# Two units of 1024 tokens, behind four units of 512: an H3 convolution layer interleaved with a squared-ReLU MLP

## The chip, the cores and the metric

The kernel runs on one core of a Trainium2 chip. The metric is the device time of one execution, in microseconds (us), as the median of several runs. The engines are named as in the profile: PE is TensorE, DVE is VectorE, ACT is ScalarE, POOL is GpSimd, SP is SyncE, which issues nearly all DMAs. "PEld" is the weight load of TensorE.

## What is computed

The reference, cut to what matters (S = 2048 tokens, D = 1024, F = 3584, everything float32):

```python
def A(u, k, v, shift_k, ssm_k, ssm_D):        # u = layernorm(x)
    k_shift = sum(k_pad[:, t:t + S] * shift_k[:, 3 - t] for t in range(4))
    kv = k_shift * v
    y = causal_conv(kv, ssm_k)                # per channel, as long as the sequence (by FFT)
    return u * (y + kv * ssm_D)
def B(u, w1, b1, w2, b2):
    return relu(u @ w1 + b1) ** 2 @ w2 + b2

x = A_q
for _ in range(2):                            # the same weights, and the same y, in both layers
    x = x + A(layernorm(x), ...)
    x = x + B(layernorm(x), ...)
```

## The kernel before

**Units.** The tokens are cut into four blocks of 512. The MLP of one layer for one block is a *unit*, and ORDER (L36) lists the eight of them as (layer, block): (0,0), (1,0), (0,1), (0,2), (1,1), (0,3), (1,2), (1,3). A float32 product is made of two rounded halves of each operand with three matmuls (mm3, L343 to L346: high by high, high by low, low by high), each 128x128 by 128x512. A *step* is one weight tile of 128x512: four mm3, or 12 matmuls. All steps stand in one list, and the program walks it (from about L2150); what is to happen beside the matmuls is hung on it: `lag.at(k, fn)` calls a function k steps later, generators (`prep_a`, `prep_rows`, `make_t`, the convolution's streams) are advanced by so much per step.

**Three sorts of unit.** A plain unit takes 112 steps (1344 matmuls): first w1 by the normalised rows of x, then relu2 (L1584), which squares and splits into rh and rl, then w2. Units 0 to 4 are plain. Unit 5, named by JU, is *joint* (add_joint, L934): the blocks (0,3) and (1,2) share each weight, as the two rows of a 2x2 block product done with 7 products instead of 8. Its first half ("ja", 98 steps) is w1 in 14 pairs of F tiles: products 1 and 2 of two pairs at a time, then products 6, 5, 7, 4, 3 from pair to pair. Product 1's bank is copied away (j_p1, L1905, tile fx) before the same banks are used on for the next product. Its second half ("jb", 98 steps) is w2 in the order JORD, with the left operands read back from HBM (r_load, r_hi, r_lo, walked by r_advance) and each finished product added into accumulators (j_evict). The sums of w1 tiles are made on the way (part_sums, L1045); the sums of w2 tiles (T) are made ahead by the generator make_t (L1599) and kept in HBM (TD). A joint unit is 196 steps (2352 matmuls). The last unit, (1,3), has a form of its own (WINO, add_wino L918): w1 in full, and 7 of 8 products of w2 within its 512 tokens; 1260 matmuls. `j_next` prepares its rows while the joint unit ends (late stage: transposes on PE, hi and lo copies, L2046 to L2049, from tiles yh).

**The convolution.** y is the same in both layers, and so is computed once, block by block, on the side. Its forward transforms (fwd_x, fwd_g; fwd_stream) are matmuls and butterflies, its products a stream (prod_stream, L528): POOL multiplies two spectra over j+1 blocks of 128 (`mult`, L532 to L534, tile cp, 128x384 to 128x1024 while unit 0 and later ones run), DVE sums over the blocks (`red`, L538, tile sm), POOL folds (fold, L683) and turns (butterfly, L686 to L689), DVE splits (L570), PE transforms back, and the result goes to HBM (yd). The stream is paced: `pace` gives each unit so much of it per step, such that block sb is done when unit WIN[sb] prepares its rows; `close_conv` forces what is left. Block 3 is not needed before unit 5, and so the convolution runs until 1700 us, in unit 4. After it make_t begins (L2380 or so).

**Rows.** prep_a and prep_b load and normalise the next unit's rows; prep_rows (L879) does so for the second block of a joint unit (layer norm, gate, layer norm), the statistics being kept in tiles rn. The bias b2 is added by POOL to the four accumulators of a unit, each 128x1024, one after the other (add_b2, L1829 to L1831).

**Weights.** They come eight steps ahead from HBM, raw (wr<-w, then split by ACT at L1103 and DVE at L1111) or as pairs split earlier (whl<-wd_m).

Of the kernel before, what the change touches and what calls it, by code (L numbers as in the profile page):

```python
# [3 lines left out]

# [22 lines left out]
FC = 7  # L27
# [30 lines left out]
JOPEN = (0, 4, 1)  # L58
JSUM = {0: ((0, 0),), 4: ((1, 1),), 5: ((0, 1),), 2: ((0, 1),), 1: ((0, 0),), 6: ((1, 1),), 3: ((1, 0),)}
J_PREP, J_SUMS, J_RATE = 22, 3, 1.1  # L60
R_LOAD, R_HI, R_LO = 8, 4, 3
W_PREP, W_EARLY, W_LATE = 90, (87, 80, 45, 38), 30
T_KEPT, T_RATE, T_AT = 10, 0.6, (0, 3, 1, 2)
WCH = (3, 3, 4, 4)
WHALF = T // 2
WORD, WORD_END = (0, 1, 3, 4, 5, 6, 2), (0, 3, 5, 6, 4, 2, 1)
WEND = {0: (), 3: (), 5: ((1, 1, 5, 0),), 6: ((1, 1, 6, 5), (2, 1, 3, 6), (2, 0, 3), (3, 1, 6, "x"), (3, 1, 1, 0)),
        4: ((1, 1, 6, 4), (1, 0, 6), (2, 1, 5, 4), (2, 1, 2, 5)), 2: ((1, 0, 2),), 1: ((1, 0, 1),)}
# [8 lines left out]
FWD_RATE = {0: 1.4, 1: 1.4, 2: 1.4, 3: 1.1, 4: 1.1, 5: 1}  # L77
# [171 lines left out]
def tile_h3_mlp(ctx: ExitStack, tc: tile.TileContext, q, kT, vT, shk, ssmT, ssmD, w1, b1, w2, b2,  # L249
# [97 lines left out]

    def hold(n):
        got = take(n)
        while not got:  # L350
            yield
            got = take(n)
        return got
# [8 lines left out]
    def fwd_x(sb, c):  # L362
# [14 lines left out]
        for _ in range(4 if sb == 1 else 7):  # L377
            yield
# [12 lines left out]
        yield  # L391
        give(o)
        yield
# [19 lines left out]
        yield  # L413
# [24 lines left out]
    def fwd_g(sb, c):  # L438
# [9 lines left out]
        if sb > PLAIN:  # L448
            hi = mkfg([P, T], F32R)
            lo = mkfg([P, T], F32R)  # L450
            A.copy(hi, raw)
            yield
            V.tensor_sub(lo, raw, hi.bitcast(F32))
            yield
            yield
            yield
# [38 lines left out]
        if sb <= PLAIN:  # L495
            yield
            yield
# [30 lines left out]
    def prod_stream():  # L528
# [3 lines left out]
        def mult(st, xt, gt, j):  # L532
            pr = cv.tile([P, CU, j + 1], F32, name="cp", bufs=3)
            G.tensor_mul(pr.rearrange("p c i -> p i c"), xt[:, 0:j + 1], gt[:, j::-1])  # L534
            st["pr"] = pr
# [4 lines left out]
        def fin(st, sm, sb, g, k):  # L540
# [24 lines left out]
            elif k == 3:  # L565
# [6 lines left out]
                if g % 2:  # L572
                    lag.at(1, fin, st, sm, sb, g, 4)
# [109 lines left out]
    def fold(E, s):  # L683
        E.tensor_add(s[:, 1:3], s[:, 1:3], s[:, 0:1].to_broadcast([P, 2, s.shape[2]]))  # L684
# [137 lines left out]
    def prep_w(l, b, lag):  # L822
        mv, r = lnx.pop((l, b))
        xT = []
        sts = [{} for _ in range(NT)]

        def early(tt, k):
            st = sts[tt]
            if k == 0:
                st["x"] = load_x(l, b, tt)  # L830
                st["y"] = pre.tile([P, D], F32, name="px", bufs=2)
                SY.dma_start(st["y"], YD[b][:, tt])
            elif k == 1:
                combine(st["x"], st.pop("y"), mv[:, tt, 0:1], r[:, tt:tt + 1])
            elif k == 2:
                st["mv"] = pre.tile([P, 1, 2], F32, name="mv2", bufs=4)
                stats(st["x"], st["mv"][:, 0])
                st["ve"], st["sd"] = rstd_a(st["mv"])
            elif k == 3:
                SY.dma_start(X1[b][:, tt], st.pop("x"))  # L840
                st["r"] = rstd_b(st["ve"], st["sd"])
                st["nr"] = pre.tile([P, 1], F32, name="nr", bufs=4)
                V.scalar_tensor_tensor(st["nr"], st["mv"][:, 0, 0:1], -1.0, st["r"], op0=OP.mult, op1=OP.mult)

        def late(tt, k):
            st = sts[tt]
            if k == 0:
                st["x"] = pre.tile([P, D], F32, name="px", bufs=2)
                SY.dma_start(st["x"], X1[b][:, tt])
            elif k == 1:  # L850
                for h in range(2):
                    sl = slice(h * 512, (h + 1) * 512)
                    A.activation(st["x"][:, sl], st["x"][:, sl], AF.Identity, bias=st["nr"], scale=st["r"])
            elif k == 2:
                if not xT:
                    xT.extend(mw.tile([P, KT, T], F32R, name=nm, bufs=1) for nm in ("xh", "xl"))
                st["o"] = []
                for kh in range(2):
                    o = ps1()
                    for c in range(4):  # L860
                        n = 4 * kh + c
                        PE.transpose(o[:, c * P:(c + 1) * P], st["x"][:, n * P:(n + 1) * P], ident)
                    st["o"].append(o.rearrange("p (k t) -> p k t", k=4))
            else:
                for kh in range(2):
                    hi, lo = (x[:, 4 * kh:4 * kh + 4, tt * P:(tt + 1) * P] for x in xT)
                    if k == 3:
                        A.copy(hi, st["o"][kh])
                    else:
                        V.tensor_sub(lo, st["o"][kh], hi.bitcast(F32))  # L870

        for tt in range(NT):
# [1551 lines left out]
```

## Time and profile before

| | us |
|---|---|
| median of 3 runs | 2679.24 |
| lowest, highest | 2675.58, 2681.99 |
| the profiled execution, its time | 2678.93 |
| its span in the trace | 2677.1 |
| PE busy | 2621.7 |
| DVE busy | 1987.5 |
| ACT busy | 1116.0 |
| POOL busy | 851.7 |
| DMA | 759.28 MB on the main queue |

The units follow one another in the trace at these times: the first convolution block until 126 us, then unit 0 (126 to 503), unit 1 (to 845), unit 2 (to 1179), unit 3 (to 1511), unit 4 (to 1828), the joint unit 5 (to 2385) and the last unit (to 2677). A row of the view by windows has the stretch, its length, then for PE, PEld, DVE, ACT and POOL the busy time with the count of instructions that fall in it, then the granted clock, the busy share of the DMA engines and GB/s. A row of the view of waits names an engine and line, what it waited for, the total in us, how many times, and the longest. A row of the view of one line has the count and the shortest, median and longest duration in ns.

### The profile page before, as it was taken

What the parts mean: (1) busy time and instruction counts of PE and PEld (TensorE: products, weight loads), DVE (VectorE), ACT (ScalarE), POOL (GpSimd) and SP (SyncE); (2) the same over time, 40 slices, a digit from 0 to 9 for tenths busy, and PEclk for the clock granted to TensorE, in tenths of its full rate; (3) what the DMA queues carried; (4) which work ended last, traced back from release to release, by engine and by line L of the source; (5) the groups of instructions that cost most, each with busy time, mean ns of one, the idle gap of its engine ahead of it and who ended that gap; (6) DMA issues with size and microseconds to landing.
All of it is one profiled execution on the core that took longest, in us unless ns stands there. A gap on an engine that the chain in (4) does not pass through costs nothing.

```text
span 2677.1 us, 36183 instructions
## 1 busy us (share of the span) xinstructions
PE 2621.7 (98%) x12400; PEld 2195.7 (82%) x12400; DVE 1987.5 (74%) x2993; ACT 1116.0 (42%) x1947; POOL 851.7 (32%) x532
## 2 busy tenths in 40 slices
PE   7999999999999999999999999999999999999999
PEld 7888787888888888888888888887787888788887
DVE  7879888789887877779777777655788674745565
ACT  4454344434444333343333422345655443345443
POOL 2336665355642645427554275100000030001000
PEclk9999999999999999999999999999999999999999
DMA  8789898689989898888987888777899988746556
GB/s 259 260 301 313 294 307 282 240 294 374 339 296 317 315 337 299 267 306 307 337 298 257 308 301 315 266 243 285 304 308 303 367 296 310 265 164 197 174 171 206
DMA packets 390680, 761.59 MB, mean 284 GB/s; under 512 B 45392, under 2 KB 160736, under 8 KB 390496
## 3 DMA queue, kind: packets, MB, share of 16 engines
q1 hardware_dynamic: 390496, 759.28, 82.4%
q8 instruction: 98, 1.61, 0.2%
q14 instruction: 86, 0.70, 0.1%
HBM read 581.92 MB, written 177.21 MB: 284 GB/s over the span
## 4 chain that ended last, share of the span: by engine, by line
PE 76%; DVE 9%; DMA 8%; issue 2%; SPq 2%; ACT 2%; POOL 1%; DVEq 0%; ACTq 0%; POOLq 0%
PE p L344 22%; PE p L345 22%; PE p L346 22%; DMA wr<-w 3%; PE p L1189 2%; PE pt L345 2%; PE pt L344 2%; PE pt L346 2%; DVE whl L1111 1%; DMA whl<-wd_m 1%; DMA cx<-xd 1%; DMA cg<-gd 0%; DVE st L705 0%; SPq L1955 0%; PE pt L429 0%
## 5 line engine op out<-in xcount | busy, mean ns | idle before, releaser
L534 POOL TENSOR_TENSOR cp<-cx,cg 128x384 f32<-128x384 f32 (+5 forms) x288 | 546.1, 1909 | 572.0 <-DVE sm L538 367.0
L344 PE MATMUL p<-xh,whl 128*128 128x512 f32 (+1 forms) x1504 | 576.8, 384 | 4.8 <-ACT fx L1907 2.9
L346 PE MATMUL p<-xh,whl 128*128 128x512 f32 (+1 forms) x1504 | 572.4, 381 | 0.8 <-POOL whl L1111 0.8
L345 PE MATMUL p<-xl,whl 128*128 128x512 f32 (+1 forms) x1504 | 572.4, 381 | 0.1
L1111 DVE TENSOR_TENSOR whl<-wr,whl 128x512 fp32r<-128x512 f32 x535 | 452.2, 858 | 95.6 <-ACT whl L1103 82.6
L1103 ACT CAST whl<-wr 128x512 fp32r<-128x512 f32 x550 | 334.7, 618 | 383.0 <-PE p L346 243.8
L344 PE MATMUL p<-whl,rh 128*128 128x512 f32 x1204 | 475.5, 395 | 3.8 <-ACT whl L1103 2.8
L345 PE MATMUL p<-whl,rh 128*128 128x512 f32 x1204 | 470.7, 391 | 1.3 <-POOL whl L1111 0.8
L346 PE MATMUL p<-whl,rl 128*128 128x512 f32 x1204 | 470.4, 391 | 0.0
L344 PEld LDWEIGHTS p<-xh,whl 128*128 128x128 f32 x1504 | 283.5, 189 | 59.5 <-ACT fx L1907 4.6
L346 PEld LDWEIGHTS p<-xh,whl 128*128 128x128 f32 x1504 | 283.1, 188 | 55.3 <-POOL whl L1111 1.0
L345 PEld LDWEIGHTS p<-xl,whl 128*128 128x128 f32 x1504 | 283.3, 188 | 52.3 <-DVE xl L1502 0.3
L344 PEld LDWEIGHTS p<-whl,rh 128*128 128x128 f32 x1204 | 227.3, 189 | 50.8 <-ACT whl L1103 3.8
L345 PEld LDWEIGHTS p<-whl,rh 128*128 128x128 f32 x1204 | 227.3, 189 | 48.1 <-DVE whl L1111 1.6
L346 PEld LDWEIGHTS p<-whl,rl 128*128 128x128 f32 x1204 | 226.9, 188 | 47.7
L1596 DVE TENSOR_TENSOR rl<-wr,rh 128x512 fp32r<-128x512 f32 x140 | 140.2, 1002 | 165.5 <-ACT rh L1591 165.5
L538 DVE TENSOR_REDUCE sm<-cp 128x128 f32<-128x384 f32 (+5 forms) x288 | 249.8, 874 | 11.4 <-POOL cp L534 11.4
L1588 ACT ACTIVATE wr<-p,b1t 128x512 f32<-128x512 f32 x138 | 95.2, 690 | 356.5 <-PE p L346 355.5
L2036 POOL TENSOR_TENSOR acc<-acc,px 128x512 f32<-128x512 f32 x8 | 11.7, 1481 | 454.0 <-DMA wr<-td 451.0
L1711 DVE TENSOR_TENSOR acc<-p,acc 128x512 f32<-128x512 f32 x152 | 99.8, 686 | 74.5 <-PE p L346 74.5
L684 POOL TENSOR_TENSOR sm<-sm 128x512 f32<-128x512 f32 x48 | 69.1, 1440 | 130.6 <-DVE sm L538 117.8
L1688 POOL TENSOR_TENSOR acc<-acc,px 128x512 f32<-128x512 f32 x6 | 7.7, 1318 | 267.6 <-DMA px<-b 267.6
(431 smaller groups left out, 4233.8 us busy)
## 6 DMA issues: line engine op xcount, KB each, us to landing
whl<-wd_m SPq DMA_DIRECT2D x334, 512.0 KB, 5.5
wr<-w SPq DMA_DIRECT2D x440, 256.0 KB, 5.4
wd_m<-whl SPq DMA_DIRECT2D x70, 512.0 KB, 6.2
wr<-td SPq DMA_DIRECT2D x104, 256.0 KB, 4.5
cx<-xd SPq DMA_DIRECT2D x48, 512.0 KB, 6.2
cg<-gd SPq DMA_DIRECT2D x48, 512.0 KB, 7.1
rh<-rd SPq DMA_DIRECT2D x84, 256.0 KB, 5.8
gd<-fg SPq DMA_DIRECT2D x72, 256.0 KB, 6.2
```

What stands on the lines that cost most here:

```text
L344: PE.matmul(o, lh, rh, start=start, stop=False, skip_group_check=skip)
L345: PE.matmul(o, lh, rl, start=False, stop=False, skip_group_check=skip)
L346: PE.matmul(o, ll, rh, start=False, stop=stop, skip_group_check=skip)
L534: G.tensor_mul(pr.rearrange("p c i -> p i c"), xt[:, 0:j + 1], gt[:, j::-1])
L538: V.tensor_reduce(sm[:, ty, jj], st["pr"], axis=AX.X, op=OP.add)
L684: E.tensor_add(s[:, 1:3], s[:, 1:3], s[:, 0:1].to_broadcast([P, 2, s.shape[2]]))
L1103: A.copy(t[:, 0], raws[n]["t"])
L1111: ENG[e[n % len(e)]].tensor_sub(t[:, 1], raws[n]["t"], t[:, 0].bitcast(F32))
L1189: PE.matmul(o, lh, r, start=start, stop=stop)
L1588: A.activation(r, st["o"], AF.Relu, bias=b1t[:, st["f"]:st["f"] + 1])
L1596: V.tensor_sub(st["lo"], st["r"]["t"], st["hi"].bitcast(F32))
L1711: V.tensor_add(accs[tt][:, d], o, accs[tt][:, d])
```

## The change

ORDER becomes (0,0), (1,0), (0,1), (0,2), (0,3), (1,1), (1,3), (1,2). Units 0 to 3 are plain as before, and behind them stand two joint units: JS = (4, 6), the blocks (0,3) with (1,1), and (1,3) with (1,2). The form of the last unit and all its functions (add_wino, prep_w, relu_w, evict_w, merge_w, store_w) are gone. In matmuls of 128x512 the main products go from 5 x 1344 + 2352 + 1260 = 10332 to 4 x 1344 + 2 x 2352 = 10080; the program's other PE instructions stay the same in number. What goes with it:

- The convolution is paced to end with unit 3 (PACE, PACE_SLACK, the forward transforms' FWD_RATE), and with it the order of its stages in steps (LAG_*).
- G_BLOCKS: POOL's multiplication is cut into pieces of at most three blocks of 128, and the fold into two additions. POOL's multiplications go from 288 to 624, all 128x256 or 128x384, and its additions of 128x512 in the fold (48) become 96 of 128x256.
- add_b2 adds 128x512 instead of 128x1024, one addition every two steps (B2_AT, B2_STEP), instead of four in a row.
- make_t starts 90 steps ahead of the first joint unit (T_RATE), while the convolution still runs, with tiles jr until the joint unit has begun.
- J_GROUP: products 1 and 2 of four pairs at a time instead of two. JORD: the order of the seven products of w2 changes. J_COMB, J_LATE: the stages of j_next, which now prepares the second joint unit's first block, are spread further. J_ROWS: prep_rows of the second joint unit's second block runs in the first one's second half.

```diff
-ORDER = [(0, 0), (1, 0), (0, 1), (0, 2), (1, 1), (0, 3), (1, 2), (1, 3)]
+ORDER = [(0, 0), (1, 0), (0, 1), (0, 2), (0, 3), (1, 1), (1, 3), (1, 2)]
-PACE_SLACK = {1: 74, 3: 10}
-PACE_TO = {1: 2}
+PACE_SLACK = 50
+PACE = (0.82, 0.98, 1.08, 1.12)
+G_BLOCKS = 3
-WINO = (7,)
-JU = 5
-WMAKE = 4
-JORD = (0, 4, 5, 2, 1, 6, 3)
+JS = (4, 6)
+JORD = (0, 1, 4, 5, 2, 6, 3)
-J_PREP, J_SUMS, J_RATE = 22, 3, 1.1
+J_SUMS = 4
+J_GROUP = 4
+J_ROWS = 37
+J_COMB = (7, 10, 16, 19)
+J_LATE = (3, 5, 6, 7)
-T_KEPT, T_RATE, T_AT = 10, 0.6, (0, 3, 1, 2)
+T_KEPT, T_AT = 14, (0, 3, 1, 2)
+T_RATE = ((-90, 0.9), (0, 0.4), (30, 1.5))
-FWD_RATE = {0: 1.4, 1: 1.4, 2: 1.4, 3: 1.1, 4: 1.1, 5: 1}
+B2_AT = 10
+B2_STEP = 2
+FWD_RATE = {0: 1.4, 1: 1.6, 2: 1.7, 3: 1.7}
...
         def mult(st, xt, gt, j):
             pr = cv.tile([P, CU, j + 1], F32, name="cp", bufs=3)
-            G.tensor_mul(pr.rearrange("p c i -> p i c"), xt[:, 0:j + 1], gt[:, j::-1])
+            n = -(-(j + 1) // G_BLOCKS)
+            cuts = [(j + 1) * k // n for k in range(n + 1)]
+            for a, e in zip(cuts, cuts[1:]):
+                G.tensor_mul(pr[:, :, a:e].rearrange("p c i -> p i c"), xt[:, a:e],
+                             gt[:, j - a:j - e if e <= j else None:-1])
...
     def fold(E, s):
-        E.tensor_add(s[:, 1:3], s[:, 1:3], s[:, 0:1].to_broadcast([P, 2, s.shape[2]]))
+        for k in (1, 2):
+            E.tensor_add(s[:, k], s[:, k], s[:, 0])
...
-        for n in range(0, NP, 2):
+        for n in range(0, NP, J_GROUP):
             for kh in range(2):
-                for p in (n, n + 1):
+                for p in range(n, min(n + J_GROUP, NP)):
...
-    def add_b2(st, accs):
-        for a in accs:
-            G.tensor_add(a, a, st["t"])
+    def add_b2(st, accs, n):
+        a = accs[n % NT][:, n // NT * T:n // NT * T + T]
+        G.tensor_add(a, a, st["t"][:, n // NT * T:n // NT * T + T])
...
-                close_conv(ORDER[u + 1][1])
+                close_conv(ORDER[u + 1][1] if u < 3 else NB - 1)
```

In three places the order of the instructions shows it. On POOL, in unit 3, the multiplications (cp, of the spectra cx and cg), a fold, a turn and the four additions of b2 (acc, px) stand like this before:

```order
L534 TENSOR_TENSOR cp<-cx,cg 128x7x128
L534 TENSOR_TENSOR cp<-cx,cg 128x8x128
L684 TENSOR_TENSOR sm<-sm 128x512
L1831 TENSOR_TENSOR acc<-acc,px 128x1024 x4
L534 TENSOR_TENSOR cp<-cx,cg 128x7x128
L688 TENSOR_TENSOR sm<-sm 128x256
L689 TENSOR_TENSOR sm<-sm 128x4x64
```

and like this, in unit 3 too, with the change:

```order
L697 TENSOR_TENSOR sm<-sm 128x256 x2
L1705 TENSOR_TENSOR acc<-acc,px 128x512
L545 TENSOR_TENSOR cp<-cx,cg 128x2x128 x2
L545 TENSOR_TENSOR cp<-cx,cg 128x3x128
L701 TENSOR_TENSOR sm<-sm 128x256
L702 TENSOR_TENSOR sm<-sm 128x4x64
L1705 TENSOR_TENSOR acc<-acc,px 128x512
L545 TENSOR_TENSOR cp<-cx,cg 128x2x128
L545 TENSOR_TENSOR cp<-cx,cg 128x3x128 x2
L1705 TENSOR_TENSOR acc<-acc,px 128x512
```

No instruction of POOL is longer than three blocks or 512 columns any more, and between two additions of b2 stand multiplications.

On DVE, in unit 3 with the change, the sums of w2 tiles (jr) now stand between the convolution's reductions (sm<-cp), the next rows' statistics (st<-px) and the eviction of an accumulator; before, they began behind the last reduction:

```order
L550 TENSOR_REDUCE sm<-cp 128x128
L402 TENSOR_TENSOR fx<-pt,fx 128x512
L1051 TENSOR_TENSOR whl<-wr,whl 128x512
L718 BN_STATS st<-px 128x6 x2
L719 BN_AGGR mv<-st 128x2
L1567 TENSOR_TENSOR jr<-jr 128x256
L1568 TENSOR_TENSOR jr<-jr 128x256
L550 TENSOR_REDUCE sm<-cp 128x128
L1570 TENSOR_TENSOR jr<-jr 128x256
L1571 TENSOR_TENSOR jr<-jr 128x256
L423 TENSOR_TENSOR fy<-pt,fx 128x8x64
```

So unit 3 takes up what units 4 and 5 did: the rest of the convolution, the rows of the joint unit and the beginning of T.

On ACT, at the start of the joint unit, a COPY to fx takes product 1 out of its bank p, and the ACTIVATE of wr from the same bank takes product 2, which the next step but one (before) has put there; before:

```order
L1907 COPY fx<-p_17588 128x512
L1103 CAST whl<-wr 128x512
L1854 ACTIVATE acc<-acc,rn 128x512 x2
L1907 COPY fx<-p_17613 128x512
L1103 CAST whl<-wr 128x512
L1854 ACTIVATE acc<-acc,rn 128x512 x2
L1902 ACTIVATE wr<-p_17588,b1t 128x512
```

and with the change:

```order
L1782 COPY fx<-p_15758 128x512
L1043 CAST whl<-wr 128x512
L1782 COPY fx<-p_15783 128x512
L1043 CAST whl<-wr 128x512
L1782 COPY fx<-p_15808 128x512
L1043 CAST whl<-wr 128x512
L1782 COPY fx<-p_15831 128x512
L1043 CAST whl<-wr 128x512
L1777 ACTIVATE wr<-p_15758,b1t 128x512
```

Between the copy of a bank and its next use there were the matmuls of one step; now there are those of three.

More of the change, by code (lines that the diff above doesn't have):

```diff
@@ L346, in mm3, with idle @@
         PE.matmul(o, ll, rh, start=False, stop=stop, skip_group_check=skip)
+    def idle(n):
+        for _ in range(n):
+            yield
     def hold(n):
@@ L376, in fwd_x @@
         V.tensor_mul(ks, ks, v4)
-        for _ in range(4 if sb == 1 else 7):
-            yield
+        yield from idle(LAG_KV[sb > 1])
         o, = yield from hold(1)
@@ L412, in fwd_x @@
         V.tensor_sub(xv[:, 1], ev, ov)
-        yield
+        yield from idle(LAG_ODD)
         give(*oa)
@@ L494, in fwd_g @@
             yield
-        if sb <= PLAIN:
-            yield
-            yield
+        yield from idle(LAG_GO[sb > PLAIN])
         give(*oa)
@@ L820, in combine @@
             V.scalar_tensor_tensor(x[:, sl], y[:, sl], r, x[:, sl], op0=OP.mult, op1=OP.add)
[L822 to L872, printed above, removed]
-            for k, d in enumerate((0, 4, 5, 7)):
-                lag.at(W_PREP - W_EARLY[tt] + d, early, tt, k)
-            for k, d in enumerate((0, 5, 7, 8, 9)):
-                lag.at(W_PREP - W_LATE + 5 * tt + d, late, tt, k)
-        return xT
@@ L1039, in room @@
     def room(w):
-        n = 3 if wsrc[w][0] == "s" and wsrc[w][3] not in parts else 1
+        n = 3 if wsrc[w][0] == "s" and wsrc[w][1::2] not in parts else 1
         return all(len(ring) + k < RAWS or ring[k - RAWS].get("freed", now[0]) < now[0] - 1 for k in range(n))
@@ L1100, in w_hi @@
         else:
-            while wsrc[n][0] == "s" and "made" not in parts[wsrc[n][3]]:
+            while wsrc[n][0] == "s" and "made" not in parts[wsrc[n][1::2]]:
                 part_sums(pend.pop(0)[1])
@@ L1603, in places @@
         def places(n):
+            if not joint_on:
+                return [ml.tile([P, 2, 256], F32, name="jr", bufs=7) for _ in range(2)]
             return [pool.tile([P, 2, 256], F32, name=nm, bufs=m) for pool, nm, m in (
```

801 lines of the change are left out of this document (352 added, 449 removed).

## The prediction

> **What bounds the kernel now.** I read the page's busy times first, then its slices, then the view by windows with one row per unit, then the waits.
>
> ```profile
> PE 2621.7 (98%) x12400; PEld 2195.7 (82%) x12400; DVE 1987.5 (74%) x2993; ACT 1116.0 (42%) x1947; POOL 851.7 (32%) x532
> ...
> PE   7999999999999999999999999999999999999999
> ...
> DVE  7879888789887877779777777655788674745565
> ...
> POOL 2336665355642645427554275100000030001000
> PEclk9999999999999999999999999999999999999999
> DMA  8789898689989898888987888777899988746556
> ```
>
> PE is busy in every slice but the first, at full clock: the time is the number of matmuls times their step, plus what PE loses in places. DVE and the DMA engines stand at eight to nine tenths in the first half, while POOL's convolution runs, and have room in the second. Now by unit (0 to 4, the joint unit, the last unit), with two stretches more:
>
> ```profile
> core 0: us, PE busy (x) PEld busy (x) DVE busy (x) ACT busy (x) POOL busy (x), PEclk, DMA share, GB/s
> 126.00:503.00 377.00, 361.62 (x1740) 304.66 (x1739) 310.13 (x456) 164.96 (x296) 195.15 (x151) 0.98 0.89 298
> 503.00:845.00 342.00, 338.93 (x1758) 290.36 (x1757) 289.06 (x419) 149.06 (x265) 157.51 (x94) 1.00 0.89 311
> 845.00:1179.00 334.00, 333.46 (x1582) 279.99 (x1581) 264.44 (x367) 124.13 (x221) 151.51 (x87) 1.00 0.88 303
> 1179.00:1511.00 332.00, 331.65 (x1558) 277.73 (x1558) 257.40 (x332) 118.51 (x209) 164.41 (x82) 1.00 0.86 300
> 1511.00:1828.00 317.00, 314.57 (x1425) 260.96 (x1424) 215.36 (x329) 102.95 (x179) 103.59 (x53) 1.00 0.82 291
> 1828.00:2385.00 557.00, 547.35 (x2420) 449.01 (x2419) 383.62 (x644) 275.16 (x477) 23.95 (x16) 0.99 0.83 290
> 2385.00:2677.00 292.00, 287.30 (x1261) 235.84 (x1259) 159.55 (x269) 129.43 (x210) 10.19 (x8) 1.00 0.58 193
> 560.00:700.00 140.00, 138.24 (x658) 115.95 (x657) 122.07 (x166) 50.48 (x92) 74.54 (x44) 1.00 1.00 354
> 2150.00:2310.00 160.00, 160.00 (x707) 132.48 (x707) 99.07 (x139) 61.97 (x109) 19.36 (x13) 1.00 0.85 301
> ```
>
> Units 1 to 3 lose next to nothing: PE is idle for 3.1, 0.5 and 0.4 us. Unit 0 takes 35 us more than unit 1 with as many matmuls, at DVE 310 of 377. The joint unit is idle for 9.65, unit 4 for 2.4 and the last one for 4.7 (of these 4.2 behind its last matmul, whose row stands below). In the last row PE does nothing but main matmuls, without a gap: 160 us over 706 or 707 of them (one is cut by the edge), **0.2266 us each**.
>
> **The change part by part.** The sum is made against the profiled run: span 2677.1, time 2678.93, so 1.8 around it; the median shown, 2679.24, is 0.3 above.
>
> *Matmuls.* 10332 main matmuls become 10080, the others stay. 252 x 0.2266 = **-57.1**. As stages: unit 4 and the last unit, 317 + 292 = 609, give way to a second joint unit.
>
> *Waits of a joint unit*, from the view of PE's waits in the joint unit:
>
> ```profile
> PE p L344 <- DVE yh L2049: 3.8, 1, 3.8
> PE p L344 <- ACT fx L1907: 2.9, 3, 1.5
> PE p L344 <- DVE px L1931: 1.2, 3, 0.7
> PE p L344 <- ACT fx L1925: 1.1, 2, 0.7
> ```
>
> The first belongs to preparing the unit behind a joint one; the second joint unit has none behind it. So the second brings 9.65 - 3.8 = 5.85 of idle, and what it replaces had 2.4 + 0.5 apart from the tail, which stays: **+2.9** (0 if only L1907's remain, +6.7 if it loses all of 9.65). J_GROUP lets the copy to fx have three steps instead of one, 8 us instead of 2.7: both units lose the 2.9 of L1907, **-5.8** (0 to -8, if L1925's go as well). J_COMB spreads the stages that end at yh; behind that wait stood the next block's first w1, and nothing else is due there: **-3** (0 to -3.8). The last product of the kernel has four evictions instead of two behind it. Its last matmul and evictions, from the timeline, and all evictions:
>
> ```profile
> 2672.66 1.39 DVE L1695 TENSOR_TENSOR acc<-p,acc 128x512 f32<-128x512 f32 x2 [3.31 <-PE p L346]
> ...
> 2672.93 0.39 PE L346 MATMUL p<-whl,rl 128*128 128x512 f32 x1
> ...
> L1711 DVE TENSOR_TENSOR acc<-p,acc 128x512 f32<-128x512 f32 x152 | 99.8, 686 | 74.5 <-PE p L346 74.5
> ```
>
> Two of 0.69 more: **+1.4**.
>
> *POOL's pieces*, with the forms that bear on their price:
>
> ```profile
> L534 POOL TENSOR_TENSOR cp<-cx,cg 128x1024 f32<-128x1024 f32 x48 | 125.1, 2606 | 130.7 <-DVE sm L538 130.7
> ...
> L534 POOL TENSOR_TENSOR cp<-cx,cg 128x512 f32<-128x512 f32 x48 | 71.8, 1495 | 15.4 <-DVE sm L538 15.4
> L684 POOL TENSOR_TENSOR sm<-sm 128x512 f32<-128x512 f32 x48 | 69.1, 1440 | 130.6 <-DVE sm L538 117.8 <-DVE rs L719 5.5 <-DMA whl<-wd_m 4.3
> L534 POOL TENSOR_TENSOR cp<-cx,cg 128x384 f32<-128x384 f32 x48 | 60.7, 1265 | 72.1 <-DMA cg<-gd 67.8 <-DVE sm L538 4.3
> ...
> L689 POOL TENSOR_TENSOR sm<-sm 128x256 f32<-128x256 f32 x49 | 43.3, 884 | 3.8
> ```
>
> A multiplication of 128x256 isn't in the trace: 0.88 by the turn of that shape, 1.03 by the line through 384 and 512; I take 0.95. The 624 pieces are 48 times seven of 384 and six of 256, 48 x (7 x 1.265 + 6 x 0.95) = 699 us where 288 took 550; the fold adds 48 x (2 x 0.9 - 1.44) = 17. POOL thus has some 165 us more in units 0 to 3 and takes over unit 4's 93: in units 1 to 3 some 80 each on 151 to 164, so 240 of 332. POOL alone bounds nothing; its price is what it does to DVE and the queue behind SP.
>
> DVE waits for POOL in this trace, whole instructions long. The view of the line that splits relu's output:
>
> ```profile
> L1596 DVE TENSOR_TENSOR rl<-wr,rh x140: 675/693/2960, 142.4 to 1787.5; 128x512 fp32r<-128x512 f32 x140
> ...
> L538 DVE TENSOR_REDUCE sm<-cp x288: 534/857/1217, 191.4 to 1689.5; 128x128 f32<-128x384 f32 x48, 128x128 f32<-128x640 f32 x48, 128x128 f32<-128x896 f32 x48
> ```
>
> The same subtraction takes 0.69 us or as much as 2.96, about a POOL instruction more, while the reduction with its one input has no such tail. The Trainium skill says why: on its page "SBUF — State Buffer" (section "Who interferes with whom" and the summary) a DVE operation with two SBUF inputs and a GpSimd operation that reads SBUF exclude one another, and the later one stands for the whole of the other; the trace agrees (0.69 against 2.96). By that rule the longest single block here would fall from about 2.3 us to about 0.6, while more POOL time lies about to be met.
>
> So shorter pieces help the latency of single results and cost in total. Unit 0 is where latency is paid, in PE's waits there:
>
> ```profile
> PE pt L429 <- DVE fx L376: 8.7, 4, 6.3
> ...
> PE pt L604 <- DVE fg L493: 2.5, 1, 2.5
> ```
>
> If all of it went, -11.2; if the 11.5 us that its share of the pieces and folds adds on POOL (unit 0 has mostly the short forms) delayed PE one for one, +11.5. I take **-4**, nearer to the gain, since POOL is idle for half of the unit.
>
> *Units 1 to 3 become denser.* Each instruction of both programs, in the order of each unit and with the trace's duration where POOL doesn't disturb it, gives DVE 238.5, 207.6 and 186.4 us before and 255.6, 229.4 and 228.1 now (convolution from unit 4, the joint unit's rows, 13 or so of 28 parts of T). With the rows' busy times that makes 306 of 342, 286 of 334 and 299 of 332: up to 0.90, and unit 0 at 0.82 of its long time is 0.91 of what its matmuls need. DMA bytes, counted from the same order, go from 107.5, 100.9 and 98.6 MB to 113.8, 113.5 and **120.9** (the window of unit 3 confirms it: 300 GB/s x 332 us = 99.6). The fastest long stretch, 560 to 700 us, moved 354 GB/s with the engines all busy, and PE lost 1.8 us in it. At that rate units 1 and 2 need 321 us, less than they have; unit 3 needs 341.5, **+9.5** on 332. I put units 1 to 3 together at **+10**, with bounds 0 and +42 (rival 2).
>
> The Trainium skill has a rule against this part: "DMA: Bandwidth & Descriptors", section "Specifications", gives an HBM limit per core of about 358 GB/s. The trace's 354 over 140 us agrees. An estimate by the page's figure is 338 us for unit 3, +6 in place of +9.5.
>
> *At nothing*, with the rows that price them without cover:
>
> ```profile
> L2036 POOL TENSOR_TENSOR acc<-acc,px 128x512 f32<-128x512 f32 x8 | 11.7, 1481 | 454.0 <-DMA wr<-td 451.0
> ...
> L705 DVE BATCH_NORM_STATS2 st<-px 128x6 f32<-128x512 f32 x32 | 20.5, 681 | 0.0
> ...
> L820 DVE SCALAR_TENSOR_TENSOR px<-px,rs 128x512 f32<-128x512 f32 x8 | 12.2, 1526 | 0.3
> L819 DVE SCALAR_TENSOR_TENSOR px<-px,mv 128x512 f32<-128x512 f32 x8 | 6.4, 802 | 0.0
> ```
>
> The 32 additions of b2 lie on POOL long before the first eviction needs the accumulators; without that cover 8 x 1.48 = 12 us per unit. prep_rows of the second joint unit runs in the first one's second half, where DVE does 99 us in 160 and DMA 301 GB/s; without cover its statistics and products, 39 us in unit 4's window with two blocks' worth, would come on top. LAG_*, rn and JORD change when, not how much.
>
> The sum: 2677.1 - 57.1 + 2.9 - 5.8 - 3 + 1.4 - 4 + 10 = 2621.5; with 1.8 around it 2623.3, and 0.3 more to the median: **2624**.
>
> **The rivals.**
>
> *2. Units 1 to 3 are bound by DMA or by the DVE-POOL exclusion.* For: unit 3's 364 GB/s at the old pace; counted by quarters, unit 1's middle 85 us ask for 411 GB/s (85 x (411/354 - 1) = +14) and unit 2's start +5, with unit 3 +28. By the exclusion, POOL and two-input DVE work of the same order together exceed the wall time in five of the twelve quarters, by 4 to 11.5 us, +42 if nothing else gives. Against: weights come eight steps (22 us) ahead, and the units had 0.9 of share already with 0.5 us idle. Time: 2614 + 28 to 2614 + 42, 2642 to 2656.
>
> *3. Slower.* The place is units 1 to 3, the mechanism that DVE (0.90) delivers the convolution's transforms or split weights later than PE takes them, as in unit 0, which paid 35 us at 0.91. Then 3 x 35 = 105 replace the 10: 2719. It decides from (2679 - 2614)/3 = 22 us per unit. Against: unit 0 also starts with everything late, its waits are on its own forward transforms, and unit 1 at 289 of 342, 0.85, paid 3.
>
> *4. The change doesn't do what it says.* T, the second block's rows or the products' operands are late in the second joint unit, so that it takes as long as the 609 us before: the 57 are not gained, 2680. Against: the joint unit ran PE for 547 of 557 with DVE at 384.
>
> *5. More.* Unit 0's pieces halve its 35 us and units 1 to 3 lose nothing: 2624 - 10 + 4 - 17 = 2601.
>
> **How the numbers follow.** The forecast 0.60 (2611 to 2641); rival 2 0.22; rival 3 0.08; rival 4 0.04; rival 5 0.06. About 0.2% (5 us) is what a measurement of this kernel can tell from no change. Faster: 0.60 + 0.22 + 0.06 = 0.88; same: rival 4, 0.04; slower: 0.08. The bounds of all terms at once would give 2601 to 2684, which they won't do together; the range leaves out rivals 3 and 4 and most of 5, and takes in rival 2 with a few us of waits in the joint units on top: 2607 to 2660.
>
> **What would show it.** Joint units of 545 to 555 us each, with L1782's wait for fx gone and no wait of 3 us or more ahead of the second; units 1 and 2 within 5 us of 342 and 334; unit 3 near 342 with a DMA share of 1.0 and the waits on whl<-wd_m or whl's split. Unit 0 under 377. Rival 2 would show as PE's waits on DMA or on DVE behind POOL in units 1 to 3, rival 3 as waits on fx and fg there, rival 4 as waits on rt, rh or td in the second joint unit. I'd be wrong in the frame if matmuls' step weren't 0.2266 any more, by a lower granted clock behind more frequent waits.

## The result, and the profile after

| | before | after |
|---|---|---|
| median, us | 2680.96 (7 runs, 2675.58 to 2683.88) | 2665.6 (7 runs, 2660.54 to 2671.58) |
| ratio, after to before | | 0.9947 (95%: 0.9933 to 0.996) |
| span of the profiled execution | 2677.1 | 2658.7 |
| PE busy | 2621.7 | 2578.0 |

Faster by half a per cent, 15 us, where 55 were forecast, and 6 us above the upper end of the range. The lines of the page that answer to those of before:

```profile
PE 2578.0 (97%) x12148; PEld 2156.2 (81%) x12148; DVE 1999.8 (75%) x3088; ACT 1159.6 (44%) x2044; POOL 961.6 (36%) x936
...
DVE  7868788778888788887989857875678666766553
...
POOL 2436666248663677754876400000300000003000
...
DMA  8789898689998999889999887978978476779682
```

PE has 252 instructions less, as planned; its busy share fell by a point, though. POOL is through with the convolution by slice 23 of 40 (26 before) and reaches seven and eight tenths ahead of that; DVE and DMA are fuller than before in the same slices. The windows, one per unit (0, 1, 2, 3 and the two joint ones):

```profile
core 0: us, PE busy (x) PEld busy (x) DVE busy (x) ACT busy (x) POOL busy (x), PEclk, DMA share, GB/s
126.00:504.00 378.00, 363.84 (x1740) 305.24 (x1740) 298.50 (x458) 164.88 (x296) 213.88 (x219) 0.98 0.89 298
504.00:869.00 365.00, 351.93 (x1806) 301.14 (x1805) 301.59 (x454) 154.05 (x276) 208.17 (x197) 0.98 0.90 310
869.00:1222.00 353.00, 344.19 (x1635) 288.24 (x1634) 288.54 (x406) 131.69 (x238) 234.70 (x231) 0.99 0.92 323
1222.00:1562.00 340.00, 328.28 (x1505) 271.35 (x1505) 297.77 (x446) 115.79 (x206) 209.97 (x216) 0.99 0.98 358
1562.00:2116.00 554.00, 544.41 (x2415) 448.05 (x2414) 389.79 (x675) 276.87 (x485) 24.62 (x16) 1.00 0.81 279
2116.00:2658.00 542.00, 537.81 (x2386) 444.61 (x2385) 316.08 (x470) 264.50 (x454) 24.38 (x16) 1.00 0.70 239
```

Within unit 3, the stretch below is as long as the one from which the prediction took 354 GB/s (560 to 700 us before); it moved 390:

```profile
1340.00:1480.00 140.00, 132.23 (x586) 107.95 (x586) 130.02 (x189) 36.42 (x68) 104.17 (x110) 0.99 1.02 390
```

Unit 0 took 377 us and takes 378, where the forecast had 4 less. The first joint unit, 554, lies within the forecast's 545 to 555, and the second, 542, is even shorter. Units 1 to 3 took 344, 334 and 330 us from first matmul to first matmul, and now take 365, 353 and 340; the prediction had allowed units 1 and 2 only 5 us more. In all three PE is idle for 9 to 13 us, and in all three its clock is under 1.00, which it was in none before. What it waits for there:

```profile
PE p L353 <- DMA whl<-wd_m: 13.4, 8, 2.8
PE pt L353 <- DVE fy L424: 11.1, 3, 6.1
PE pt L354 <- DVE fx L402: 2.1, 1, 2.1
PE p L353 <- ACT wr L1529: 1.5, 1, 1.5
```

The waits are for weights that come late by DMA, and for DVE: a bank that it has not emptied (fy), an operand that it has not finished (fx). These are the shapes that rival 2 named, though waits on fx are also the sign that rival 3 gave. The account below goes by the *loss* of a unit: the time between successive starts of matmuls in the trace, less the usual step of each (0.227 us for 512 columns, 0.120 for 256, 0.111 for 128), summed over the unit of the profiled execution. It holds the waits and the slower clock, and leaves the matmuls out.

| stage | loss before | loss after | what it adds to the time |
|---|---|---|---|
| matmuls, 252 fewer | | | -57.1 |
| unit 0 | 36.8 | 37.5 | +0.7 |
| unit 1 | 4.6 | 20.9 | +16.3 |
| unit 2 | 1.0 | 13.6 | +12.6 |
| unit 3 | 0.8 | 16.3 | +15.5 |
| first joint unit | 15.6 | 13.5 | -2.1 |
| second joint unit, for unit 4 and the last | 5.1 | 0.8 | -4.3 |
| sum | | | -18.4 |

That is the difference of the spans, 2658.7 - 2677.1. The profiled execution of the changed kernel is the fastest of its seven, 5 us under the median. So the saving arrived in full, and 44.4 us of it were lost again in units 1 to 3. The question for the experiments is what they are lost to.

### The profile page after: what moved, and what is told of

Its sections match the earlier page's. It is cut to its first block, busy times and chain, and to the rows that moved or that the text cites. A ratio compares the mean times of both kernels' runs of the same rounds, so it can differ in the third digit from the quotient of the medians.

```text
span 2658.7 us, 36587 instructions
## 1 busy us (share of the span) xinstructions
PE 2578.0 (97%) x12148; PEld 2156.2 (81%) x12148; DVE 1999.8 (75%) x3088; ACT 1159.6 (44%) x2044; POOL 961.6 (36%) x936
## 4 chain that ended last, share of the span: by engine, by line
PE 63%; DMA 17%; DVE 10%; SPq 2%; POOL 2%; ACT 2%; issue 2%; DVEq 0%; ACTq 0%; POOLq 0%
PE p L353 17%; PE p L354 17%; PE p L355 17%; DMA whl<-wd_m 3%; PE pt L354 2%; PE pt L353 2%; DMA cg<-gd 2%; PE pt L355 2%; DMA wr<-w 2%; PE p L1129 2%; POOL cp L545 2%; DVE whl L1051 1%; DVE sm L550 1%; DMA xd<-fy 1%; DMA wd_m<-whl 1%
## 5 line engine op out<-in xcount | busy, mean ns | idle before, releaser
L545 POOL TENSOR_TENSOR cp<-cx,cg 128x384 f32<-128x384 f32 (+1 forms) x624 | 638.7, 1057 | 360.9 <-DMA cg<-gd 198.9
L353 PE MATMUL p<-xh,whl 128*128 128x512 f32 (+1 forms) x1168 | 448.6, 384 | 8.7 <-DMA whl<-wd_m 6.4
L354 PE MATMUL p<-xl,whl 128*128 128x512 f32 (+1 forms) x1168 | 443.1, 379 | 0.1
L355 PE MATMUL p<-xh,whl 128*128 128x512 f32 (+1 forms) x1168 | 442.9, 379 | 0.0
L353 PE MATMUL p<-whl,rh 128*128 128x512 f32 x896 | 357.2, 399 | 9.5 <-DMA whl<-wd_m 7.0
L354 PE MATMUL p<-whl,rh 128*128 128x512 f32 x896 | 353.1, 394 | 2.5 <-DVE whl L1051 1.9
L355 PE MATMUL p<-whl,rl 128*128 128x512 f32 x896 | 352.4, 393 | 0.0
L353 PEld LDWEIGHTS p<-xh,whl 128*128 128x128 f32 x1168 | 221.5, 190 | 50.5 <-DMA whl<-wd_m 5.6
L355 PEld LDWEIGHTS p<-xh,whl 128*128 128x128 f32 x1168 | 220.9, 189 | 41.7
L354 PEld LDWEIGHTS p<-xl,whl 128*128 128x128 f32 x1168 | 221.3, 190 | 39.4 <-DVE xl L1442 0.3
L353 PEld LDWEIGHTS p<-whl,rh 128*128 128x128 f32 x896 | 170.4, 190 | 46.4 <-DMA whl<-wd_m 8.9
L354 PEld LDWEIGHTS p<-whl,rh 128*128 128x128 f32 x896 | 170.3, 190 | 38.5 <-DVE whl L1051 3.9
L697 POOL TENSOR_TENSOR sm<-sm 128x256 f32<-128x256 f32 x96 | 85.1, 898 | 66.3 <-DVE sm L550 66.2
L353 PE MATMUL p<-whl,xl 128*128 128x512 f32 x272 | 105.9, 389 | 0.3 <-DMA whl<-wd_m 0.3
L355 PE MATMUL p<-whl,xl 128*128 128x512 f32 x272 | 105.8, 389 | 0.0
```

The lines of the kernel that those rows point to most:

```text
L353: PE.matmul(o, lh, rh, start=start, stop=False, skip_group_check=skip)
L354: PE.matmul(o, lh, rl, start=False, stop=False, skip_group_check=skip)
L355: PE.matmul(o, ll, rh, start=False, stop=stop, skip_group_check=skip)
L545: G.tensor_mul(pr[:, :, a:e].rearrange("p c i -> p i c"), xt[:, a:e], gt[:, j - a:j - e if e <= j else None:-1])
L697: E.tensor_add(s[:, k], s[:, k], s[:, 0])
```

## The experiments

Three theories to start with. **H**: the convolution's forward transforms are ticked (advanced) faster, and the loads of the filter (fg<-ssmT) land too late for ACT and DVE, which stand at the head of their queues for them. **D**: the DMA engines are full. **X**: DVE stands for POOL. A fourth, **V**, is DVE's own amount of work. H came from the view of the tile fg in units 1 to 3 of the changed kernel; before, there was a single such wait, of 3.4 us:

```profile
who waited for it (us, times):
...
  ACT fg L463: 38.3, 7
```

The losses of units 1 to 3 and of the first joint unit, in the profiled execution of each run, and the ratio to before of the timed runs:

| run | unit 1 | unit 2 | unit 3 | sum | joint | median us | ratio (95%) |
|---|---|---|---|---|---|---|---|
| before | 4.6 | 1.0 | 0.8 | 6.4 | 15.6 | 2680.96 | |
| after | 20.9 | 13.6 | 16.3 | 50.8 | 13.5 | 2665.6 | 0.9947 (0.9933 to 0.996) |
| e1_gwait | 23.8 | 18.1 | 20.5 | 62.4 | 15.4 | 2677.24 | 0.9994 (0.9986 to 1.0003) |
| e2_tlate | 19.9 | 14.7 | 4.3 | 38.9 | 38.4 | 2671.41 | 0.9973 (0.9963 to 0.9984) |
| e3_whole | 24.1 | 17.2 | 25.0 | 66.3 | 12.1 | 2679.41 | 0.9997 (0.9988 to 1.0005) |
| e4_group2 | 19.6 | 14.8 | 16.9 | 51.3 | 13.0 | 2662.03 | 0.993 (0.9918 to 0.9941) |
| e5_pool | 9.9 | 5.3 | 12.9 | 28.1 | 15.7 | 2641.14 | 0.9854 (0.9839 to 0.9869) |
| e6_dma | 11.5 | 3.0 | 9.3 | 23.8 | 14.2 | 2637.26 | 0.9841 (0.9827 to 0.9854) |
| e7_dve | 13.8 | 12.2 | 15.6 | 41.6 | 15.7 | 2658.2 | 0.9922 (0.9908 to 0.9935) |
| e8_tmid | 18.1 | 12.3 | 7.7 | 38.1 | 25.5 | 2665.14 | 0.9938 (0.9925 to 0.995) |
| e9_both | 1.5 | 1.1 | 0.3 | 2.9 | 14.0 | 2615.34 | 0.9759 (0.9746 to 0.9772) |
| e10_four | 19.7 | 14.8 | 19.6 | 54.1 | 12.7 | 2664.14 | 0.9946 (0.9933 to 0.9958) |
| e11_raw | 22.6 | 14.6 | 23.8 | 61.0 | 13.3 | 2671.72 | 0.9966 (0.9953 to 0.9979) |
| e12_mix | 20.6 | 14.6 | 11.0 | 46.2 | 11.2 | 2652.42 | 0.9894 (0.9877 to 0.9912) |

A loss is that of one execution, and executions of one kernel differ by several us, so a difference of a few us between two losses means little where the medians don't bear it out.

### e1_gwait: three ticks more between the filter's load and its split

```diff
-        for _ in range(FWD_WAIT):
+        for _ in range(FWD_WAIT + 3 * (sb > PLAIN)):
```

> Theory H (late filter loads): units 1 to 3 lose time because the forward transforms are ticked faster (1.6 and 1.7 instead of 1.4 per step) with the same four ticks between a filter's load and its split, so that ACT and DVE stand at the head of their queues for fg<-ssmT. With three ticks more, ACT's 38 us of idle time before L463 in units 1 to 3 falls under 8, PE's waits on fy (11 us) go, and the time falls by 12 to 20 us to about 2650. Theory D (the DMA engines are full): the same bytes move, unit 3 stays at 340 and units 1 and 2 gain at most 3 each: 2660 or more. Theory X (DVE stands for POOL's many pieces): no change, 2665.

12 us slower. The waits that H named went: PE's on fy are gone, and ACT's idle time before L463 is down from 38 us to under 1. Others came, in the view of PE's waits in units 1 to 3:

```profile
PE p L353 <- DMA whl<-wd_m: 12.1, 11, 2.9
PE pt L354 <- DVE yl L582: 8.2, 5, 3.0
PE pt L354 <- DVE fx L402: 7.4, 4, 2.8
```

H's gain isn't there: the load of the filter was where a shortage showed, and with this wait out of the way other things are late, and the loss even grows. The edit doesn't make the loads earlier, though; it makes the splits later (the last at 1293 us instead of 1261), and so moves the transforms too. What speaks against H more plainly comes from e6 below: with the ticks as they were and other loads left out, ACT's wait before L463 falls from 38.3 to 8.7 us. So these loads are late with the rest. This wait could have been read as the cause from the trace alone.

### e2_tlate: the sums of w2 tiles wholly in the joint unit

```diff
-T_RATE = ((-90, 0.9), (0, 0.4), (30, 1.5))
+T_RATE = ((0, 1.5), (30, 1.5))
```

> The sums of w2 tiles begin with the first joint unit at 1.5 per step, so some 17 MB of unit 3's 121 and 52 DVE subtractions (22 us) go from unit 3 into the first half of the joint unit. Theory D: unit 3 falls from 340 to about 331 at 105 MB, its waits on whl<-wd_m (6.5 us) go; the joint unit pays 0 to 4 of it: 2657 to 2661. Theory H: unit 3's one wait on fy (1.9) may go, 2663 to 2666. Theory X: DVE has 22 us less in unit 3, 2660 to 2664, by shorter waits on ACT and DVE instead of DMA.

Unit 3 gave back its 12 us, as D expected. The joint unit paid 25 for it, far more than any theory allowed; most of the added waits are for ACT and DVE, on L1777 alone 10.7 us instead of 2.4. So its first half has no room for T's work at this rate. Without T unit 3 loses 12 us less of its 16, and T is worth that where it stands.

### e3_whole: POOL's multiplications in one piece

```diff
-G_BLOCKS = 3
+G_BLOCKS = 8
```

> POOL multiplies in whole instructions again (288 instead of 624), the rest stays. Theory X (the pieces' sum of time blocks DVE): POOL's busy time falls by 90 to 150 us and units 1 to 3 gain 10 to 20: 2648 to 2656. Theories H and D: within 4 of 2665. If what counts is the length of a single block: slower by 4 to 12, 2670 to 2677, with unit 0's wait on fx longer again by 3.

14 us slower, somewhat more than the 4 to 12 that the theory of the longest block gave: the pieces, which the prediction booked as a cost in total, pay. Busy times of this run's page, and the line that splits relu's output, after and with whole instructions:

```profile
PE 2580.5 (97%) x12148; PEld 2158.2 (81%) x12148; DVE 2068.6 (77%) x3088; ACT 1159.0 (43%) x2044; POOL 881.5 (33%) x600
```

```profile
L1536 DVE TENSOR_TENSOR rl<-wr,rh x112: 673/693/1577, 142.3 to 1521.4; 128x512 fp32r<-128x512 f32 x112
```

```profile
L1536 DVE TENSOR_TENSOR rl<-wr,rh x112: 674/692/2909, 142.3 to 1536.6; 128x512 fp32r<-128x512 f32 x112
```

POOL works 80 us less, and DVE, with the same instructions, is busy for 69 us more. The longest of the same subtractions takes 2.91 us with whole instructions and 1.58 with pieces, against 0.69 undisturbed. So what counts here is how long a single block lasts more than POOL's sum of time. The Trainium skill's rule ("SBUF — State Buffer", "Who interferes with whom") has the later instruction stand for the whole of the earlier one. The trace agrees as far as it goes: the longest subtraction exceeds 0.69 us by 2.2 and by 0.9, in neither run by more than POOL's longest multiplication (2.9 and 1.6 us).

### e4_group2: products 1 and 2 of two pairs at a time

```diff
-J_GROUP = 4
+J_GROUP = 2
```

> Products 1 and 2 of two pairs at a time again. By the sum's term, PE's waits on the copy to fx come back in both joint units, 2 x 2.9: 2671. The rival is that the copies were late for other reasons (they are still waited for 4.3 us with groups of four): no change, 2664 to 2667.

Not slower: 0.993 against 0.9947, with overlapping intervals. Both joint units lose what they lost (13.0 and 0.4 us against 13.5 and 0.8). The 5.8 us that the sum gave to the groups aren't there; the rival expectation, no change, holds, and the time is even 2 us under its bounds.

### e5_pool, e6_dma and e7_dve: one resource's work left out at a time

POOL's multiplications (e5):

```diff
-            cuts = [(j + 1) * k // n for k in range(n + 1)]
+            cuts = [(j + 1) * k // n for k in range(n + 1)] if j < 2 * BT else [0, 1]
...
-            st["pr"] = pr
+            st["pr"] = pr if j < 2 * BT else pr[:, :, 0:1].to_broadcast([P, CU, j + 1])
```

> Leaves out part of the convolution: for blocks 2 and 3 POOL multiplies only the first 128 columns of each product, and DVE's reduction reads these over and over, in the same number of elements; loads, DVE and PE stay. Theory X (DVE stands for POOL, and POOL is late): units 1 to 3, which lose 50 us of PE in the changed kernel, lose under 15, and the time falls to 2630. Theory D (the DMA engines are full): their loss stays over 40, 2655 to 2668. Theory V (DVE's own amount of work, with in-order queues): between, as DVE is no longer stretched by POOL but does the same work: loss 25 to 35, 2640 to 2650.

The spectra's loads (e6), POOL then reading one block over and over:

```diff
-                SY.dma_start(t, src[g, :, :nb])
+                SY.dma_start(*((t, src[g, :, :nb]) if sb < 2 else (t[:, 0:1], src[g, :, 0:1])))
```

> Leaves out part of the convolution's loads: for blocks 2 and 3 each load of spectra brings one block of 128 instead of 6 or 8, some 75 MB less over units 1 to 3; POOL multiplies that block over and over in the same number of elements, DVE and PE stay. Theory D: with about 25 MB of 113 to 121 gone from each unit, their loss falls from 50 to under 15, 2630. Theory X: the loss stays over 40 but for the waits on whl<-wd_m (13 us), 2648 to 2665. Theory V: as X.

DVE's sums (e7):

```diff
-            V.tensor_reduce(sm[:, ty, jj], st["pr"], axis=AX.X, op=OP.add)
+            pr = st["pr"] if sm_sb[0] < 2 else st["pr"][:, :, 0:1]
+            V.tensor_reduce(sm[:, ty, jj], pr, axis=AX.X, op=OP.add)
```

> Leaves out part of the convolution's sums: for blocks 2 and 3 DVE reduces only the first 128 columns of each product, about 0.2 instead of 0.8 to 1.2 us, some 150 us less over units 1 to 3; loads, POOL and PE stay. Theory V (DVE's amount of work is what PE waits for): units 1 to 3 lose under 15 instead of 50, 2630. Theory D: the loss stays over 40, 2655 to 2668. Theory X: DVE meets POOL as before with its two-input work and POOL is released sooner: loss 35 to 50, 2650 to 2665.

None of the three brought the loss under 15, so no theory holds alone. Without POOL's multiplications 28.1 us remain, without the loads 23.8, with DVE's sums cut 41.6. By its number e5 fits V, which had 25 to 35 for it. But e7 takes as much of DVE's time away, 888 to 766 us in the three units, and gains only 9 where V had over 35; and its interval (0.9908 to 0.9935) still touches that of the changed kernel. The first two differ in what is left. Units 1 to 3 without the multiplications, by windows and by PE's waits:

```profile
505.00:859.00 354.00, 347.12 (x1806) 297.82 (x1805) 267.35 (x454) 154.54 (x276) 98.08 (x129) 1.00 0.91 320
859.00:1204.00 345.00, 341.51 (x1637) 286.41 (x1636) 254.49 (x406) 131.12 (x238) 92.40 (x123) 1.00 0.95 330
1204.00:1540.00 336.00, 325.99 (x1502) 269.43 (x1501) 253.49 (x445) 115.05 (x206) 71.59 (x104) 1.00 0.99 363
```

```profile
PE p L353 <- DMA whl<-wd_m: 12.1, 9, 2.7
PE pt L353 <- DVE fy L424: 4.5, 3, 2.7
```

and without the loads:

```profile
507.00:863.00 356.00, 348.17 (x1808) 298.96 (x1807) 309.27 (x454) 154.46 (x276) 213.45 (x197) 0.99 0.77 253
863.00:1205.00 342.00, 340.23 (x1633) 285.95 (x1632) 287.74 (x405) 131.56 (x237) 235.20 (x231) 1.00 0.77 251
1205.00:1538.00 333.00, 327.37 (x1504) 271.72 (x1503) 307.03 (x446) 115.57 (x206) 216.99 (x216) 0.99 0.86 292
```

```profile
PE pt L353 <- DVE fy L424: 6.1, 2, 4.8
PE pt L354 <- DVE yl L584: 2.8, 4, 1.5
PE pt L354 <- DVE fx L402: 2.0, 2, 1.0
PE p L353 <- DMA whl<-wd_m: 2.0, 1, 2.0
```

With POOL relieved, DVE's busy time in the three units falls from 888 to 775 us with the same instructions, and PE waits for weights, at DMA shares up to 0.99. With the bytes gone, DVE is as busy as ever (904), the DMA share is 0.77 to 0.86, and PE waits for DVE above all. Two shortages, each with its own waits.

Which of DVE's instructions became shorter in e5 says what POOL does to it. Two groups of units 1 to 3, the reduction and the split of weights, after and then in e5:

```profile
L550 DVE TENSOR_REDUCE sm<-cp 128x128 f32<-128x768 f32 (+2 forms) x195 | 194.3, 1000 | 5.6 <-POOL cp L545 5.6
L1051 DVE TENSOR_TENSOR whl<-wr,whl 128x512 fp32r<-128x512 f32 x153 | 145.2, 950 | 12.2 <-ACT whl L1043 12.1
```

```profile
L550 DVE TENSOR_REDUCE sm<-cp 128x128 f32<-128x768 f32 (+2 forms) x195 | 194.6, 1003 | 2.6 <-POOL cp L545 2.6
L1051 DVE TENSOR_TENSOR whl<-wr,whl 128x512 fp32r<-128x512 f32 x153 | 115.7, 758 | 18.0 <-ACT whl L1043 17.9
```

The reduction, with one input, takes as long in both, and so does the eviction acc<-p,acc, which reads a bank of PE and one tile (0.68 and 0.69 us). The split, with two tiles as inputs, goes from 0.95 us to 0.76, and that of relu's output from 0.93 to 0.73. And in the changed kernel DVE's reductions waited only 5.6 us for POOL's products. So what POOL cost DVE is that it held these instructions up, not that its results came late.

### e8_tmid: T half in unit 3

```diff
-T_RATE = ((-90, 0.9), (0, 0.4), (30, 1.5))
+T_RATE = ((-60, 0.6), (0, 0.6), (30, 1.4))
```

> T begins 60 steps ahead of the joint unit at 0.6 per step instead of 90 at 0.9, and goes on at 0.6 and 1.4: about 9 of the 17 MB leave unit 3. Where unit 3 is bound by bytes and the joint unit's start by T's work beside it (T wholly late gave unit 3 back 12 us and cost the joint unit 25): unit 3 gains 6 to 8, the joint unit loses 3 to 10, 2660 to 2668. If the joint unit's cost comes only from the rate of 1.5 in its first 30 steps: it loses under 3, 2656 to 2661.

Unit 3 gained 9, the joint unit lost 12: the time stays, as the first expectation had it, though both amounts are a little over its own. T's rate in the joint unit's first 30 steps was 0.6, and the cost came nevertheless.

### e9_both: multiplications and loads left out together

The edits of e5 and e6 in one kernel.

> Leaves out both at once, POOL's multiplications but for the first 128 columns and the spectra's loads but for one block of 128, for blocks 2 and 3; DVE and PE stay. Each alone took units 1 to 3 from 50.8 us of loss to 28 (POOL) and 24 (loads). If the two add up (each resource makes its own waits): the loss falls to 0 to 8, near the 6.4 of the three units before the change, 2615 to 2622. If both act on the same waits (either relieves the same late instruction): 18 to 24 remain, 2630 to 2636. If DVE's own amount is what is left: 8 to 15.

2.9 us of loss, less than the 6.4 of before. Leaving out POOL's multiplications took away 22.7, the loads 27.0, both 47.9: over the three units they add up, and nothing of note is left for DVE's own work or for H, whose ticks are as in the changed kernel. Unit by unit they don't, in the one execution that each profile shows. In unit 1 the two single gains make 20.4 and both together 19.4; in unit 2, 18.9 and 12.5, so either alone does most of it; in unit 3, 10.4 and 16.0, so there both had to go. In ratios: 0.9947 - 0.0093 - 0.0106 gives 0.9748, measured 0.9759 (0.9746 to 0.9772). By windows, units 1 to 3:

```profile
505.00:851.00 346.00, 345.17 (x1808) 297.04 (x1807) 269.88 (x454) 153.93 (x276) 103.04 (x129) 1.00 0.79 261
851.00:1191.00 340.00, 339.53 (x1633) 286.00 (x1632) 256.48 (x405) 130.97 (x237) 93.10 (x123) 1.00 0.79 252
1191.00:1515.00 324.00, 323.82 (x1505) 270.80 (x1504) 255.39 (x446) 114.85 (x206) 75.36 (x104) 1.00 0.89 300
```

DVE at 0.75 to 0.79, DMA at 0.79 to 0.89, PE without a gap at full clock. The total, 2615, is where the change would be without the loss.

### e10_four: pieces of up to four blocks

```diff
-G_BLOCKS = 3
+G_BLOCKS = 4
-J_GROUP = 4
+J_GROUP = 2
```

> Pieces of up to four blocks (128x512) instead of three, and groups of two pairs as in the earlier run of that. POOL then has 480 multiplications instead of 624, some 40 us less work, and its longest one is 1.5 us instead of 1.27. If the sum of POOL's time counts: 3 to 6 faster than the groups of two alone (2662), so 2656 to 2660. If the length of a block counts, as whole instructions were slower by 14: 2 to 5 slower, 2664 to 2667.

0.9946 against 0.993 for the groups of two alone, with overlapping intervals: no gain from fewer pieces, and a loss can't be told from none.

### e11_raw: fewer bytes, more splits

```diff
-RAW_ONE = {}
+RAW_ONE = {2: (4, (0,)), 3: (3, (0,))}
```

> A quarter to a third of the weights of units 2 and 3 come raw (256 KB) and are split by ACT and DVE, instead of as split pairs (512 KB): 6.8 and 6.3 MB less, for 26 and 23 splits more of 0.62 us on ACT and 0.69 us on DVE. If bytes are the scarcer: the waits on whl<-wd_m (11.7 us in the two units) fall by half, 2654 to 2661. If DVE is as scarce: waits on whl's split take their place, 2664 to 2672.

6 us slower, though the interval still touches that of the changed kernel (0.9933 to 0.996). The waits on weights fell by more than half over units 1 to 3, and DVE's took their place and more:

```profile
PE pt L353 <- DVE fy L424: 12.4, 4, 6.2
PE pt L354 <- DVE yl L582: 8.3, 4, 3.9
PE p L353 <- DMA whl<-wd_m: 6.2, 4, 2.8
```

This is the second expectation: where both are scarce, one couldn't be paid with the other.

### e12_mix: groups of two, T at 0.6 in unit 3

```diff
-J_GROUP = 4
+J_GROUP = 2
-T_RATE = ((-90, 0.9), (0, 0.4), (30, 1.5))
+T_RATE = ((-90, 0.6), (0, 0.4), (30, 1.5))
```

> Groups of two pairs (2662 by themselves) and T at 0.6 instead of 0.9 per step in unit 3: 5.8 MB and a third of T's DVE work there go to the joint unit, whose first 30 steps keep the rate of 0.4. If unit 3's loss falls with its bytes and DVE work as it did by 12 for the whole 16.8 MB, unit 3 gains 4; if the joint unit pays only for T beside its first products, it loses under 2: 2658 to 2661. If every us taken from unit 3 is paid again in the joint unit, as when all or half of T was moved: 2662 or more.

2652.42, where 2658 to 2661 was expected; ratio 0.9894 (0.9877 to 0.9912), clear of the changed kernel's interval and of that with groups of two alone. In the profiles, against groups of two alone, unit 3 has 5.9 us less of loss and the joint unit 1.8 less. A third of what was moved before bought half the gain in unit 3, and cost nothing. That the joint unit's early steps keep their rate fits this, but no run changes that alone. It is the fastest complete version here.

## Why the prediction was wrong

- **Matmuls, -57.1.** Right: 252 fewer at 0.227 us each, and with the loss out of the way (e9, 65 us under before) none of them is missing.
- **Joint units.** The forecast was -5.9 for the first (groups and spreading) and about 0 for the second against what it replaced, with +1.4 at the end. Measured: -2.1 and -4.3; the last matmul starts 4.4 us before the end, 4.2 before, so the two evictions more don't show. J_GROUP's -5.8 was wrong: with groups of four the wait on L1782 is gone, as forecast, but that on L1800, the other copy to fx, went from 1.1 us (L1925 before) to 3.4; with groups of two (e4) the two take 0.6 and 0.7, and the loss is the same. The wait on yh fell from 3.8 to 2.1.
- **Unit 0, -4.** Measured +0.7, and 36.2 us of loss with whole instructions. Pieces do nothing there, neither for nor against.
- **Units 1 to 3, +10, bounds 0 and +42. This is the step that failed.** Measured +44.4. Three things were wrong in it. First, the two parts of rival 2, bytes (+28) and the DVE-POOL exclusion (+42), were treated as two views of one case, and +10 was taken; e5, e6 and e9 show two shortages, both there at once: 27.0 us go with the loads, 22.7 with POOL's multiplications, 47.9 with both. Second, the bytes were held against the mean rate of a whole unit, by which units 1 and 2 had room (321 us of need): they lost 21 and 14 us at 310 and 323 GB/s. And 354 GB/s is no limit, though the prediction found it confirmed: a stretch of unit 3 as long as the one they were read from moved 390, and PE was idle for 8 us of it. That a unit with 0.9 of share had 0.5 us of idle before was taken for slack; with 12% more bytes (100.9 to 113.5 MB) and POOL's added work it lost 13.6. Third, no term stood for the clock, which took about 13.5 of the 50.8 us (below); the prediction names it only as a sign that its frame is wrong.
- **The pieces.** POOL's time rose by 110 us where 165 were worked out (a piece of 128x256 takes 0.90 us, one of 384 1.19), but that this costs in total was wrong in sign: e3. The longest block, put at about 0.6 us, was 0.9 by relu's split (1.58 less 0.69).
- **Rival 2** is what happened, with 0.22, and its price of 2642 to 2656 was too low by 10. Rivals 4 and 5 didn't happen; of rival 3 there were waits on fx, but not its price, and e9 leaves nothing for it once POOL and the loads are relieved. Unit 3's 340 us and DMA share of 0.98 are as the forecast had them, but the 340 in part by luck: its loss rose by 15.5 us, not 9.5, while its matmuls, without the loss, take 324 us instead of 329. T makes some 12 us of that loss (e2); this overlaps with the shares of e5 and e6 and can't be added to them.

What stays open: how the two shortages meet within a unit, since they add up over three units and not in each; no run was profiled often enough to tell. And why e1 lost 12 us more, and not the same.

## What to carry to other kernels

Work that is taken off the end of a kernel and put beside other work has to be held against every shared resource of the place where it goes, and the shortages weighed together, not the worst one taken: here relieving either left half of the loss. A unit that loses nothing at a DMA share of 0.88 need not have room for a tenth more. The name in a wait is where a shortage shows: taking that wait away tells whether it is also the cause, and leaving out one resource's work at a time, then two, tells what is. Where one engine's instruction holds up another's, as POOL's did DVE's, long ones can be worth cutting even if their sum grows.

## What the runs showed of the hardware that was not expected

A wait of under 3 us can cost PE twice its length. The timeline of the changed kernel at a late weight in unit 1, and the windows around it:

```profile
661.47 0.80 PE L353 MATMUL p<-whl,rh 128*128 128x512 f32 x1 [2.79 <-DMA whl<-wd_m]
662.07 0.63 PE L354 MATMUL p<-whl,rh 128*128 128x512 f32 x1
662.49 0.63 PE L355 MATMUL p<-whl,rl 128*128 128x512 f32 x1
```

```profile
657.00:662.00 5.00, 2.21 (x9) 1.56 (x8) 2.05 (x3) 0.00 (x0) 4.92 (x7) 0.88 1.05 331
662.00:667.00 5.00, 5.00 (x14) 3.87 (x13) 0.00 (x0) 0.24 (x1) 2.44 (x3) 0.50 1.08 394
667.00:672.00 5.00, 5.00 (x27) 4.39 (x27) 4.59 (x8) 2.63 (x6) 2.00 (x2) 0.93 0.90 279
```

After 2.79 us of idle the granted clock is 0.50 for the next 5 us, and a window that holds 22 matmuls of 512 columns at full clock holds 14 instructions. The starts of matmuls from 658 to 668 us lose 5.9 us, half of it behind the wait. Not every such wait does this: behind one of 2.76 us, at 990 us in unit 2, the clock stayed full:

```profile
993.00:998.00 5.00, 5.00 (x28) 4.36 (x29) 3.02 (x4) 3.01 (x6) 5.00 (x6) 1.00 1.01 383
```

Over units 1 to 3 the part of the loss that falls on matmuls with no idle time just before the next one is 6.8 + 3.8 + 2.9 = 13.5 us; before it was 1.3. The granted clocks of 0.98, 0.99 and 0.99 over these units come to the same size, some 14 us by estimate. The Trainium skill ("TensorE: Matmul & The Clock Gate", "What's actually happening") has the clock at half after an idle window of about 3.4 us, and the window runs freely; here 2.79 us sufficed in one place and 2.76 did not in another.
